# A second DRAM scratch holds v in float32 for units 1 to 3 of a block-sparse attention and FFN kernel, and the order of all engines is searched anew

## The chip, the cores and the metric

One core of one Trainium2 chip runs the whole program. The metric is the device time of one execution in microseconds; the kernel before was timed in three executions, and one execution was profiled.

## The reference

Attention of 4 batches, 8 heads, 768 tokens and head size 64, restricted to blocks of 32 tokens: a query block sees itself and its two neighbours, the first and the last block, and three sampled blocks of its own; the first and the last block see everything. Sampled blocks may repeat one another or a block that is seen anyway, and then count once. The result, as 3072 tokens by 512, goes through a two-layer network with an ELU between 512 to 2048 and 2048 to 512.

```python
scores = scale * np.matmul(q, k.transpose(0, 1, 3, 2))
mask = np.abs(blk_i - blk_j) <= window
mask = mask | (blk_i == 0) | (blk_j == 0) | (blk_i == n_blocks - 1) | (blk_j == n_blocks - 1)
...
        for kb in sampled_blocks[qb]:
            mask[qb * block:(qb + 1) * block, kb * block:(kb + 1) * block] = True
scores = np.where(mask, scores, -1000000000.0)
scores = scores - np.max(scores, axis=-1, keepdims=True)
attn = np.exp(scores)
attn = attn / (np.sum(attn, axis=-1, keepdims=True) + 1e-09)
out = np.matmul(attn, v)
...
x = out.transpose(0, 2, 1, 3).reshape(B * S, H * D)
h = x @ w_in
g = np.where(h > 0.0, h, alpha * (np.exp(np.minimum(h, 0.0)) - 1.0))
return g @ w_out
```

## The kernel before

**Units.** The batches are taken in two pairs. A unit is 128 tokens: two query blocks of both batches of a pair. Each pair has 12 units, the first of which holds the first and the last block; 24 units in all. Unit 0 (the code's `nat`) attends to all keys and goes in four parts of two heads each. Units 1 to 3 take their scores in float32, and units from 4 on work in float16 pairs: an f32 number is held as a high and a low half, and a product is three f16 matmuls (high by high, high by low, low by high).

**v.** `first_values` loads v of the first pair in three pieces of two tiles (`in_v_dram` into the room `wo`, 512 KB a tile), splits it into high and low halves in a tile `VT` (casts for the highs, L607 on DVE for the lows, scaled by 32, with columns of ones that give the row sums), and stores that as rows of 4160 bytes into a DRAM scratch `vd` (L681). A unit's two `VT` tiles are then loaded back from `vd`: the rows of the first and last block (32 partitions each), the window (96 rows), and an indirect DMA from GpSimd that gathers the 96 rows of the three sampled blocks by the index table `idx`. The tile of spare room is called `GR` in the trace and serves unit 1, the `VT` rooms serve units 0, 2 and 3 and what follows. Sampled rows that must not count are pointed by `idx` at a row of zeros in the scratch.

**p.** Unit 0 multiplies an f32 transpose of exp's output with v as it was loaded (64 columns a product). For units 1 to 3 the transposed p is split into high and low halves, some of the lows by a matmul that subtracts the high in PSUM (`pm`, for the first `LP[u]` tiles) and a copy, the others by a subtraction on DVE; the product with v (L1076) is f16, of 130, 66 or 64 columns.

**Weights.** The 16 tiles of 1 MB of the two layers go from DRAM into staging rooms (L548, L552; the list `STAGE`), and each is turned into high and low halves: a cast (ACT or DVE), a merge on DVE (L563), a second cast, and a subtraction on GpSimd or DVE (L570). The rooms `wi` and `wo` are where the finished halves stay too; k and v as loaded lie in the halves of `wo`. The kernel runs both layers of units 0 to 3 together (`ffn_two`: layer 1 is L1173, layer 2 is L1199), tile by tile of the weights, and of the later units pair by pair of units (`ffn`).

**What sets the order.** Nothing is issued by hand. Every step is put down in a `Plan` as an operation with a cost on each engine that can run it, a DMA cost, a due time (`prio`) and buffers out of rooms of a fixed number; a list scheduler in the program then fixes engine and order. A table of numbers, `RANK`, shifts due times, says how many weight loads wait for which mark (`HOLD`), and which tiles take which form (`LP`, `AP`, `LX`). All DMAs but the gathers, instruction fetches and the like are issued by SP in one queue, so that what stands ahead of a load in that queue, and waits, holds it up.

## Time and profile before

| what | value |
|---|---|
| three executions | 725.29, 733.63, 734.4 us (median 733.63) |
| profiled execution, its own time | 729.91 us |
| its span, from the first to the last instruction | 728.2 us |
| busy: PE, DVE, ACT, POOL | 679.6, 444.5, 449.9, 161.9 us |
| mean granted TensorE clock | 0.968 |
| moved by DMA | 123.18 MB, mean 169 GB/s |

The own time lies 1.7 us above the span, and 3.7 us under the median. Busy times are counted over the whole span, in which stages follow one another: attention of units 0 to 3 with the preparation of keys, values and weights (up to about 124 us), then a long stage in which layers of one pair of units run beside the attention of the next.

### The profile page before, as it was taken

To read this page: it belongs to the slowest core of one execution; us is meant where nothing else is said; L and a number is where in the kernel's file an instruction comes from. 1 tells how busy PE (TensorE), PEld (TensorE's weight loads), DVE (VectorE), ACT (ScalarE), POOL (GpSimd) and SP (SyncE) were. 2 spreads that over 40 slices of the span, in tenths; PEclk is the share of its full clock that TensorE was granted. 3 is DMA by queue.
4 is the path that set the end of the run, shared out by engine and by line. 5 is a ranking of instruction groups with operands and counts; after the bars stand their busy time and mean duration, and the time that the engine had idled before them with its cause. 6 is when DMAs were issued, how large, how long until landed. Compare 5 with 4: busy or idle time off the path is not lost.

```text
span 728.2 us, 23487 instructions
## 1 busy us (share of the span) xinstructions
PE 679.6 (93%) x9637; PEld 456.5 (63%) x9637; DVE 444.5 (61%) x882; ACT 449.9 (62%) x872; POOL 161.9 (22%) x357
## 2 busy tenths in 40 slices
...
PEclk9777978999999999999999999999999999999999
...
GB/s 211 259 321 240 284 282 196 237 182 212 177 193 163 152 199 203 164 202 187 135 139 181 184 201 142 173 219 122 104 150 203 149 198 135 145 60 15 16 1 29
DMA packets 213500, 123.18 MB, mean 169 GB/s; under 512 B 180560, under 2 KB 197072, under 8 KB 213008
## 3 DMA queue, kind: packets, MB, share of 16 engines
...
HBM read 76.98 MB, written 13.21 MB: 124 GB/s over the span
## 4 chain that ended last, share of the span: by engine, by line
PE 81%; DMA 10%; DVE 3%; ACT 2%; issue 1%; POOL 1%; POOLq 1%; another core or an unknown queue 0%; SPq 0%; DVEq 0%; ACTq 0%
PE h L1173 32%; PE o L1199 29%; PE av L1076 6%; DMA VT<-vd,idx 3%; PE s L1199 3%; PE s L996 2%; DMA VT<-vd 2%; PE s L987 2%; DMA wi<-in_moe_w_out_dram 2%; DMA GR<-vd 1%; PE av L1199 1%; PE warm L449 1%; DMA wo<-in_v_dram 1%; PE s L975 1%; PE s L503 1%
## 5 line engine op out<-in xcount | busy, mean ns | idle before, releaser
L1173 PE MATMUL h<-xT,wi 128*128 128x256 f16 x2304 | 264.7, 273 | 4.8 <-DVE FE L1181 4.3
L1173 PEld LDWEIGHTS <-wi 128*128 128x128 f16 x2304 | 221.9, 98 | 43.0 <-issue 8.6
L1199 PE MATMUL o<-wo,GR 128*128 128x512 f16 x1008 | 230.4, 379 | 1.7 <-ACT ro L405 1.7
L1199 PEld LDWEIGHTS <-GR 128*128 128x128 f16 x1152 | 108.9, 98 | 125.8 <-issue 6.4
L927 POOL COPY kG<-kT 128x128 int32 x264 | 91.0, 382 | 232.0 <-PE s L996 103.0
L1181 DVE SCALAR_TENSOR_TENSOR FE<-h,FE 128x512 f32<-128x512 f32 x96 | 66.0, 687 | 65.7 <-ACT FE L1186 65.7
L1013 DVE TENSOR_REDUCE m<-s 128x2 f32<-128x512 f32 x120 | 73.6, 648 | 35.5 <-PE s L996 20.0
L1184 ACT ACTIVATE FE<-h 128x512 f32<-128x512 f32 x96 | 56.8, 592 | 42.7 <-PE h L1173 31.6
L1191 DVE TENSOR_TENSOR GR<-FE,GR 128x512 f16<-128x512 f32 x93 | 66.1, 711 | 26.2 <-ACT GR L405 25.1
L797 DVE TENSOR_TENSOR p<-e,p 128x512 f16<-128x512 f32 x81 | 55.6, 690 | 39.0 <-ACT p L405 36.4
L761 ACT ACTIVATE e<-s,m 128x256 f32<-128x256 f32 x176 | 72.1, 475 | 9.1 <-DVE p L797 7.3
L880 POOL DMA_INDIRECT VT<-vd,idx x42 | 43.7, 1040 | 139.4 <-PE av L1076 107.7
L405 ACT ACTIVATE kG<-kT 128x384 f32<-128x384 f32 (+1 forms) x88 | 55.3, 678 | 25.7 <-PE s L996 14.2
L1186 ACT ACTIVATE FE<-FE,gs 128x512 f32<-128x512 f32 x96 | 69.4, 723 | 2.1
L1076 PEld LDWEIGHTS <-pT 128*32 128x32 f16 (+1 forms) x3432 | 41.9, 101 | 29.1 <-issue 26.9
L405 ACT ACTIVATE GR<-FE 128x512 f16<-128x512 f32 x64 | 40.2, 628 | 28.8 <-DVE FE L1181 28.7
L1076 PE MATMUL av<-VT,pT 128*32 128x66 f16 (+3 forms) x3288 | 47.3, 207 | 9.0 <-DMA VT<-vd,idx 6.9
L405 ACT ACTIVATE p<-e 128x512 f16<-128x512 f32 x70 | 43.6, 625 | 15.4 <-DMA pT<-p 15.3
L405 ACT ACTIVATE ro<-o 128x512 f32<-128x512 f32 x20 | 11.9, 597 | 58.0 <-PE o L1199 57.9
L987 PE MATMUL s<-kG,qT 64*32 64x256 f32 x704 | 27.2, 393 | 1.1 <-DVE pT L791 0.6
L405 ACT ACTIVATE kT<-s 128x1024 f16<-128x1024 f16 (+1 forms) x16 | 14.6, 914 | 20.9 <-PE s L503 11.5
L407 DVE COPY low<-av 128x192 f32<-128x192 f32 x28 | 10.0, 355 | 27.9 <-PE av L1076 25.3
...
## 6 DMA issues: line engine op xcount, KB each, us to landing
...
```

The lines of the kernel that those rows point to most:

```text
L405: nc.scalar.activation(dst, src, AF.Copy, scale=scale)
L761: nc.scalar.activation(e32.ap[:, y, :], s.ap[:, y, :], AF.Exp, bias=m.ap[:, 6 + y : 7 + y], scale=SC, accum_out=m.ap[:, 2 + y : 3 + y] if ...
L797: plan.add(LO, rank + 1, margin=mo, fn=lambda e: ENG[e].tensor_tensor(p.ap[:, 1, :], got(), p.ap[:, 0, :], op=ALU.subtract), r=[e32, p], w ...
L927: nc.gpsimd.tensor_copy(dst[:, :, r * W : (r + 1) * W], src[:, :, bass.ds(at[r], W)])
L1013: nc.vector.tensor_reduce(m.ap[:, at + i.start : at + i.stop], ss[c].ap[:, i], axis=AX.X, op=ALU.max, negate=True)
L1076: nc.tensor.matmul(av[half].ap[rs, at : at + w], lhsT=pts[d].ap[:, pl * 4 + y * 2 + z, rs], rhs=room[:, z, x, h * VW + v0 : h * VW + v0 + ...
L1173: nc.tensor.matmul(h.ap[:, a, :], lhsT=w[:, wl, cs], rhs=x.ap[:, xl, cc, :], start=(n == 0), stop=(n == 3 * NCC - 1))
L1181: nc.vector.scalar_tensor_tensor(e32.ap, h.ap, -IH * GS, e32.ap, op0=ALU.mult, op1=ALU.min)
L1184: plan.add({"ACT": 0.6}, p0, lambda e: nc.scalar.activation(e32.ap, h.ap, AF.Exp, scale=IH), r=[h], new=[e32], name=f"a1{U}.{f2}")
L1186: plan.add({"ACT": 0.72}, p0, lambda e: nc.scalar.activation(e32.ap, e32.ap, AF.Relu, bias=gs_col, scale=-GS), r=[e32], w=[e32], name=f"a2 ...
L1191: plan.add(LO, p0, margin=mo, fn=lambda e: ENG[e].tensor_tensor(g.ap[:, 1], e32.ap, g.ap[:, 0], op=ALU.subtract), r=[e32, g], w=[g], name= ...
L1199: nc.tensor.matmul(o.ap, lhsT=g.ap[:, gl, f % 2, m * P : (m + 1) * P], rhs=wo[:, part, wl, (f % 2) * DM : (f % 2 + 1) * DM], start=(f == 0 ...
```

## The change

- `raw_values` loads v and stores it at once, as float32, in a second scratch `vr` of 384 rows of 8 KB: a row is two tokens of both batches, all heads. Six stores of 512 KB follow the loads in SP's queue.
- Units 1 to 3 load their tiles from `vr`: two edges of 16 rows, a window of 48 rows, a gather of 48 rows by a new table `pair`, all of 8 KB. Their p is transposed and copied as float32 only (`pf`), without halves, and the product with v is float32, 192 matmuls of 64 columns over the three units in place of 480 of float16.
- What must not count is masked in the scores: one matmul with one row (bf16, K = 1) for each 32 queries adds either 0 or -1e30 per key block (`never`, `once`) before the scores, 48 of them in all. Row sums come from exp's accumulator.
- The tables for this are made by some 26 more small DVE operations at the start; `pair` stands beside `idx`.
- The split of v for `vd` (`first_values`) goes behind unit 0 in due time; its highs may go to POOL, its lows stay on DVE.
- k is staged in the rooms `wi` instead of halves of `wo`. Unit 0's scores wait for the keys of their own head pair only, its odd parts use other PSUM banks (`o`, `av`, `h`), and its maxima are combined by one reduction.
- `RANK` is searched anew, with new keys: `VR`, `VP`, `VW`, `AE`, `MT`, `LATE`, `FX`.

```diff
@@ -21,15 +21,16 @@
 WINDOW = 1
 
 RANK = {
-    "K": -1408.04, "Z": 990.23, "VL": 323.4, "Q": [1459.32, 294.42, 1902.98, -915.37, 340.37,
-    -247.43, 21.55, 1498.28, 151.89], "AT": [-1283.19, 1037.72, -509.33, 271.53, 54.11, 1021.44,
...
+    "K": 138.1, "Z": -56.04, "VL": 54.81, "VR": 368.88, "Q": [109.82, 906.62, -138.61, 751.86,
+    253.1, 41.87, 432.83, 499.33, 227.65], "AT": [339.57, -227.94, 84.04, 317.22, 14.82, 102.85,
...
+    "BACK": 1.72, "AHEAD": 17.2, "T": 36.02, "LEAD": 96.31, "V1": 106.51, "K1": -283.79, "MU":
+    5.06, "MI": 10.61, "MJ": -7.07, "MV": -2.76, "MP": -31.65, "AP": [0, 0, 0, 0], "AQ": 22.41,
+    "VP": 611.21, "VW": 536.9, "AE": -32.96, "MT": 216.47, "LATE": [-12.75, -6.78, -21.79],
+    "FX": {},
 }
...
+    NF, NPE = 4, 4
+    NEVER = 1.0e30
...
-    cols = const([1, NPAIR, (NB - 2) * NR], I32, "cols")
+    cols = tabs[0:1, 0:NC].rearrange("p (g n) -> p g n", g=NPAIR)
+    pair = tabs[:, NC : NC + NU2]
+    ONE = slice(P // 2, P // 2 + 1)
+    never = tabs[ONE, 0 : NU2 * (NR + 5) // 2].bitcast(BF16).rearrange("p (a b) -> p a b", b=NR + 5)
+    once = tabs[ONE, NU2 * (NR + 5) // 2 : NU2 * (NR + 5) // 2 + BLK // 2].bitcast(BF16)
+    nc.gpsimd.memset(once, 1.0)
...
+        nc.vector.tensor_tensor(d3, few[ONE], me[ONE, 1 : 1 + NU2].unsqueeze(2).to_broadcast([1, NU2, NR]), op=ALU.subtract)
...
+                nc.vector.tensor_tensor(d3[:, :, g], few[ONE, :, g], few[ONE, :, r], op=ALU.not_equal)
+                nc.vector.tensor_tensor(ok3[:, :, g], ok3[:, :, g], d3[:, :, g], op=ALU.mult)
+        nc.vector.memset(never, 0.0)
+        nc.vector.memset(never[:, 0, NR + 2 : NR + 3], -NEVER)
+        nc.vector.tensor_scalar(never[:, :, 0:NR], ok3, -1.0, NEVER, op0=ALU.add, op1=ALU.mult)
...
+        nc.vector.tensor_scalar(pair, w6, gk, None, op0=ALU.add)
...
-    STAGE = [(wi, 6), (wi, 4), (wi, 2), (wo, 6), (wo, 4), (wi, 6), (wi, 4), (wo, 6), (wo, 4), "g2",
+    STAGE = [(wi, 6), (wi, 4), (wi, 2), (wi, 6), (wi, 4), (wo, 6), (wi, 6), (wi, 4), (wo, 4), "g2",
...
-            s = halves[2 * hp + x]
+            s = wi_room[2 * hp + x]
...
-    def first_values(a, js, prio, load, write):
+    def raw_values(a, js, load):
+        for x in range(2):
+            s, t = staged(js[x], v[x], a, load, f"v0.{a}")
+            v_raw.append((s, t))
+
+            def put(e, x=x, s=s):
+                nc.sync.dma_start(
+                    vr.ap[a * P : (a + 1) * P, x * 2 * DM : (x + 1) * 2 * DM], s.ap.bitcast(F32))
+            new = (a, x) == (0, 0)
+            mark["vr"] = plan.add({"SP": 0.43}, RANK["VR"] + a, put, r=[s], new=[vr] if new else [], w=[] if new else [vr],
+                     dma=1.45, name=f"v2.{a}", pk=128)
+
+    def first_values(a, prio, write):
         def slot():
-            assert next_slot() == a
-            return VT[:, 2 * a : 2 * a + 2].rearrange("p c b (h x) -> p c b h x", h=H)
+            i = next_slot()
+            in_room["v", i] = None
+            return VT[:, 2 * i : 2 * i + 2].rearrange("p c b (h x) -> p c b h x", h=H)
         n = Buf("VT", slot)
         plan.add({"POOL": 0.5}, prio - 3, lambda e: nc.gpsimd.memset(
             n.ap.rearrange("p c b h x -> p (c b h) x")[:, :, D : D + 2], 1.0), new=[n], name=f"v10.{a}", port=False)
         for x in range(2):
-            s, t = staged(js[x], v[x], a, load, f"v0.{a}")
-            v_raw.append((s, t))
+            s, t = v_raw[2 * a + x]
             for c in range(2):
                 split(prio, s, n, lambda x=x, c=c: n.ap[:, c, x, :, 0:D],
-                      lambda x=x, c=c: n.ap[:, c, x, :, D + 2 :], VS, False, f"v0.{a}", t[:, :, c, :], mh=RANK["MV"])
+                      lambda x=x, c=c: n.ap[:, c, x, :, D + 2 :], VS, False, f"v0.{a}", t[:, :, c, :], mh=RANK["MV"],
+                      cost=({**CAST, "POOL": 1.0}, 0.69))
...
                 nc.sync.dma_start(
                     vd[0].ap[row : row + 2 * (p1 - p0), :].rearrange("(p c) e -> p (c e)", c=2),
                     n.ap[p0:p1].rearrange("p c b h x -> p (c b h x)"))
-            mark["vs"] = plan.add({"SP": 0.43}, write, put, r=[n], w=[vd[0]], dma=2.9 * (p1 - p0) / P, name=f"vs0.{a}",
+            plan.add({"SP": 0.43}, write, put, r=[n], w=[vd[0]], dma=3.2 * (p1 - p0) / P, name=f"vs0.{a}",
                      pk=256 * (p1 - p0) // P)
...
                         start=i == 0, stop=i == 3)
             tp = rank + 2
-            plan.add({"PE": 0.9}, tp, turn, r=[e32], new=[pt], code=8, name=f"pt{u}.{n}p")
-            if sums:
-                plan.add({"ACT": 0.6, "DVE": 0.66}, tp, lambda e: scaled(e, flat(pT.ap).bitcast(F32), flat(pt.ap)),
-                         r=[pt], new=[pT], margin=RANK["MP"], name=f"pf{u}.{n}", port=False)
-                return pT
...
+                        if in_room.get(("v", vt.slot)) != "raw":
+                            in_room["v", vt.slot] = "raw"
+                            for a, n in enumerate((0, NB - 1)):
+                                nc.sync.dma_start(
+                                    tile_[(NR + a) * HB : (NR + a + 1) * HB], vr.ap[n * HB : (n + 1) * HB, :])
+                        nc.sync.dma_start(tile_[(NR + 2) * HB :], vr.ap[(i - 1) * HB : (i + 2) * HB, :])
+                        return
...
-                plan.add({"SP": 1.5 if whole else 0.6}, tv, load, r=[vd[g]], new=[vt], dma=2.45 if whole else 1.5,  slack=RANK["SLACK"][2], name=f"vt{u}", nd=3 if whole else 1)
+                cost = (1.9 if whole else 1.15) if whole_f else 2.7 if whole else 1.62
+                plan.add({"SP": 1.5 if whole else 0.6}, tv, load, r=[vr if whole_f else vd[g]], new=[vt], dma=cost, slack=RANK["SLACK"][2], name=f"vt{u}", nd=3 if whole else 1)
 
                 def gather(e, i=i, vt=vt):
+                    if whole_f:
+                        n = NR * BLK // 2
+                        nc.gpsimd.indirect_dma_start(
+                            room32(vt.slot)[0:n], None, vr.ap, bass.IndirectOffsetOnAxis(ap=pair[0:n, i - 1 : i], axis=0))
+                        return
...
-                mark["vt", u] = plan.add({"POOL": 1.0}, tv, gather, r=[vd[g]], w=[vt], dma=1.65, slack=RANK["SLACK"][2], name=f"vg{u}")
...
+            ss = [buf(tag, [P, 2, 256], F32, ps) for tag in (("o", "av", "h") if nat and part % 2 else ["s"] * len(tiles))]
...
                 if wide_k:
                     q32 = flat(qT.ap).bitcast(F32).rearrange("p (h t) -> p h t", h=H // 2)
+                    for y in range(2 if whole_f else 0):
+                        for j, (rs, x) in enumerate(groups):
+                            nc.tensor.matmul(
+                                ss[y].ap[rs].rearrange("p i (z n t) -> p (i z) n t", z=2, t=BLK // 2), lhsT=once,
+                                rhs=never[:, i0 + j % 2 - 1].unsqueeze(1).unsqueeze(3).to_broadcast([1, 4, NR + 5, BLK // 2]),
+                                start=True, stop=False)
...
+                                kk, dst = kG32[rows, part, j % 2, 2 * i + x, :], ss[y].ap[rs, i, :]
+                                if whole_f:
+                                    kk = kk.rearrange("p (t z) -> p z t", z=2)
+                                    dst = dst.rearrange("p (z t) -> p z t", z=2)
                                 nc.tensor.matmul(
-                                    ss[y].ap[rs, i, :], lhsT=q32[rows, 2 * part + i, rs],
-                                    rhs=kG32[rows, part, j % 2, 2 * i + x, :], start=True, stop=True)
+                                    dst, lhsT=q32[rows, 2 * part + i, rs], rhs=kk, start=not whole_f, stop=i == 1 or not whole_f)
...
-            plan.add({"PE": 1.3 if nat else 1.1 if sp else 0.9 if wide_k else 0.7}, at_s, wide if sp else scores,
-                     r=[qT, *kT_any, *([kT_head[part]] if nat else kT_head), *kin[part : part + 1]],
-                     new=ss, code=20 if nat else 72 if sp else 32 if wide_k else 96, name=f"s{u}.{part}")
+            if nat:
+                for one in range(2):
+                    plan.add({"PE": 1.2 if one else 0.43}, at_s, lambda e, wide=wide, one=one: wide(e, turns=turns[:4] if one else turns[4:]),
+                             r=[qT, kT_head[part]], new=[] if one else ss, w=ss[:2] if one else [], code=16 if one else 4, name=f"s{u}.{part}")
...
+            if nat:
+                plan.add({"DVE": 0.42}, at_s + 0.5, lambda e, mm=mm, ss=ss: nc.vector.tensor_reduce(
+                    mm.ap[:, 2:3], ss[2].ap[:, 0:1], axis=AX.X, op=ALU.max, negate=True), r=[ss[2]], new=[mm],
+                    name=f"mx{u}.{part}", port=False)
+                plan.add({"PE": 0.43}, at_s + 0.4, lambda e, wide=wide: wide(e, turns=[(1, 2, 2, 1)]),
+                         r=[qT, kT_head[part]], w=[ss[2]], code=4, name=f"s{u}.{part}")
...
+                            nc.vector.tensor_reduce(
+                                m.ap[:, 6:8], m.ap[:, 0:6].rearrange("p (y c) -> p y c", c=3), axis=AX.X, op=ALU.min)
+                            return
...
-                sums = Buf(None, None) if nat else None
+                sums = Buf(None, None) if whole_f else None
+                if whole_f and not nat and c == 0:
+                    total = buf("r", [P, 4], F32)
...
+                        if whole_f:
                             for z in range(2):
-                                for rs, x in groups:
+                                for j, (rs, x) in enumerate(groups):
+                                    raw = v_raw[2 * k + x][1] if nat else room32(vin[j % 2].slot).rearrange(
+                                        "p (b h c d) -> p b h c d", b=2, h=H, c=2)[:, x]
                                     nc.tensor.matmul(
                                         av[half].ap[rs, at : at + D],
                                         lhsT=flat(pts[d].ap).bitcast(F32).rearrange("p (i t) -> p i t", t=P)[:, y * 2 + z, rs],
-                                        rhs=v_raw[2 * k + x][1][:, h, z, :], start=begin, stop=(d, y, z, 1) == end)
+                                        rhs=raw[:, h, z, :], start=begin, stop=(d, y, z, 1) == end)
...
+                    if whole_f:
                         nc.vector.tensor_scalar(r.ap, r.ap, PS * 1e-9, 1.0 / VS, op0=ALU.add, op1=ALU.mult)
                         nc.vector.reciprocal(r.ap, r.ap)
...
     zero_rows(RANK["Z"])
     for a in range(NB // 8):
-        first_values(a, (2 * a, 2 * a + 1), RANK["W"], RANK["VL"] + a, RANK["W"])
+        raw_values(a, (2 * a + 2, 2 * a + 3), RANK["VL"] + a)
...
+            plan.group = "vs"
+            for a in range(NB // 8 if u == 0 else 0):
+                first_values(a, RANK["VP"], RANK["VW"])
+            plan.group = "w"
```

SP's queue, from the second half of v's way to DRAM up to the first loads of tiles. Before (`vd_505` is the scratch of halves, `ST` a room with zero rows; `wi<-in_moe...` are weights):

```order
L681 DMA vd_505<-VT 128x4160
L681 DMA vd_505<-VT 112x4160
L681 DMA vd_505<-VT 16x4160
L552 DMA wi<-in_moe_w_out_dram 128x2x2047
L548 DMA wi<-in_moe_w_in_dram 128x4x1023
L872 DMA VT<-vd_505 32x2080
L873 DMA VT<-vd_505 32x2080
L874 DMA VT<-vd_505 96x2080
```

After (`vr_352` is the new scratch, `vd_590` the old one; `wi<-in_k_dram` are keys):

```order
L716 DMA vr_352<-wo 128x1024
L676 DMA wi<-in_k_dram 128x6x128 x2
L716 DMA vr_352<-wo 128x1024 x5
L800 DMA st_553<-in_q_dram 64x8x64 x2
L800 DMA st_572<-in_q_dram 64x8x64 x2
L639 DMA vd_590<-ST 32x2080
L932 DMA GR<-vr_352 16x2048 x2
L934 DMA GR<-vr_352 48x2048
L741 DMA vd_590<-VT 128x4160
L741 DMA vd_590<-VT 112x4160 x2
L741 DMA vd_590<-VT 16x4160 x2
```

The loads of the spare tile `GR` stood behind all stores of halves and behind weight tiles; now they stand behind the stores of raw v, two loads of q and the rows of zeros, and the stores of halves come after them.

The same queue where the last tiles of v for unit 3 and the first of unit 4 are loaded. Before:

```order
L552 DMA GR<-in_moe_w_out_dram 128x2x2047
L548 DMA wo<-in_moe_w_in_dram 128x4x1023
L874 DMA VT<-vd_505 96x2080 x2
L740 DMA st_1919<-in_q_dram 64x8x64 x2
L740 DMA st_1942<-in_q_dram 64x8x64 x2
L740 DMA st_1960<-in_q_dram 64x8x64 x2
L548 DMA wi<-in_moe_w_in_dram 128x4x1023
L702 DMA st_2136<-in_v_dram 128x8x64
L874 DMA VT<-vd_505 96x2080 x2
```

After:

```order
L934 DMA VT<-vr_352 48x2048
L939 DMA VT<-vd_590 32x2080
L940 DMA VT<-vd_590 32x2080
L941 DMA VT<-vd_590 96x2080
L594 DMA wi<-in_moe_w_in_dram 128x4x1023 x2
L598 DMA wo<-in_moe_w_out_dram 128x2x2047
L939 DMA VT<-vd_590 32x2080
L940 DMA VT<-vd_590 32x2080
L941 DMA VT<-vd_590 96x2080
```

Weights, q and window loads alternated; now whole tiles of `vd` (32, 32 and 96 rows) follow one another for unit 4 and on, with three weights between.

DVE, within unit 0's parts (`m` are maxima, `s`, `o`, `av`, `h` PSUM banks, `pT` transposed p). Before:

```order
L1013 TENSOR_REDUCE m_566<-s_542 128x2
L1013 TENSOR_REDUCE m_566<-s_544 128x1
L1013 TENSOR_REDUCE m_566<-s_543 128x2
L1013 TENSOR_REDUCE m_566<-s_544 128x1
L1027 TENSOR_TENSOR m_566<-m_566 128x2
L1028 TENSOR_TENSOR m_566<-m_566 128x2
L1035 TENSOR_SCALAR m_566<-m_566 128x2
L563 SCALAR_TENSOR_TENSOR wi<-wi,ZB 128x1024
L1044 TENSOR_TENSOR r_538<-m_566 128x2
L570 TENSOR_TENSOR wi<-wi 128x1024
```

After:

```order
L418 COPY pT_446<-h_435 128x512
L418 COPY pT_457<-h_441 128x512
L1094 TENSOR_REDUCE m_473<-h_462 128x1
L654 SCALAR_TENSOR_TENSOR VT<-wo,VT 128x8x64
L1107 TENSOR_REDUCE m_473<-o_460 128x2
L1107 TENSOR_REDUCE m_473<-av_461 128x2
L1107 TENSOR_REDUCE m_473<-h_462 128x1
L1094 TENSOR_REDUCE m_516<-s_480 128x1
L1130 TENSOR_REDUCE m_473<-m_473 128x2
L1107 TENSOR_REDUCE m_516<-s_478 128x2
L1141 TENSOR_SCALAR m_473<-m_473 128x2
```

The merge and the subtraction of a weight tile stood between the maxima of one part; now the low halves of v and copies of p stand there, and the maxima of two parts interleave.

## Rows read from the trace of the kernel before

**Rows 1.** The page: busy time of PE, and its granted clock in 40 slices.

```profile
PE 679.6 (93%) x9637; PEld 456.5 (63%) x9637; DVE 444.5 (61%) x882; ACT 449.9 (62%) x872; POOL 161.9 (22%) x357
...
PEclk9777978999999999999999999999999999999999
```

**Rows 2.** Windows by stage: per engine busy us and instructions, clock, DMA share, GB/s.

```profile
20.00:72.00 52.00, 33.37 (x394) 22.89 (x389) 30.73 (x70) 26.27 (x60) 10.38 (x21) 0.74 1.05 277
72.00:124.00 52.00, 38.39 (x822) 24.25 (x819) 36.47 (x76) 40.42 (x77) 18.07 (x43) 0.84 0.93 259
124.00:180.00 56.00, 55.56 (x598) 40.22 (x597) 51.42 (x75) 44.29 (x75) 20.38 (x26) 1.00 0.87 213
262.00:700.00 438.00, 432.39 (x6396) 295.21 (x6395) 262.63 (x529) 278.57 (x538) 81.20 (x189) 1.00 0.77 147
```

**Rows 3.** The chain that ended last: start, us, what; its longest DMA steps.

```profile
20.11 6.60 DMA wo<-in_v_dram
...
38.99 14.21 DMA wi<-in_moe_w_out_dram
53.23 16.73 DMA VT<-vd
69.97 10.81 DMA GR<-vd
...
101.35 9.87 DMA VT<-vd,idx
```

**Rows 4.** Timeline of PE, 0 to 140 us.

```profile
22.48 1.57 PE L956 MATMUL s<-kT,qT 64*64 64x256 f32 x20 [1.41 <-ACT qT L405]
...
39.56 1.62 PE L1064 MATMUL av<-wo,pT 128*64 128x64 f32 x48
...
111.25 2.15 PE L1076 MATMUL av<-VT,pT 128*32 128x130 f16 x103 [3.91 <-DMA VT<-vd,idx]
...
123.69 5.41 PE L1173 MATMUL h<-xT,wi 128*128 128x256 f16 x48
```

**Rows 5.** Timeline of DVE, 0 to 125 us.

```profile
6.98 0.18 DVE L481 TENSOR_TENSOR odd<-odd 128x24 f32<-128x24 f32 x1
...
21.79 0.69 DVE L607 SCALAR_TENSOR_TENSOR VT<-wo,VT 128x512 f16<-128x512 f32 x1
...
58.88 1.22 DVE L563 SCALAR_TENSOR_TENSOR wi<-wi,ZB 128x1024 int32<-128x1024 int32 x1
...
69.93 1.29 DVE L1013 TENSOR_REDUCE m<-s 128x2 f32<-128x512 f32 x2 [1.08 <-PE s L987]
...
72.21 0.42 DVE L1101 TENSOR_TENSOR x<-av,r 128x256 f32<-128x256 f32 x1 [0.51 <-PE av L1064]
```

**Rows 6.** Timeline of ACT, 8 to 140 us.

```profile
44.12 1.34 ACT L405 ACTIVATE ZB<-wi 128x1024 f16<-128x1024 bf16 x1 [4.40 <-DMA wi<-in_moe_w_in_dram]
45.34 0.66 ACT L756 ACTIVATE FE<-s,m 128x512 f32<-128x512 f32 x1
```

**Rows 7.** Windows by what the DMA queues move; columns as in rows 2.

```profile
11.00:14.00 3.00, 3.00 (x60) 3.00 (x58) 0.00 (x0) 2.17 (x4) 0.00 (x0) 1.00 1.17 294
42.00:50.00 8.00, 3.86 (x26) 2.77 (x28) 2.61 (x3) 5.52 (x12) 0.00 (x0) 0.61 1.01 391
57.50:79.50 22.00, 18.90 (x264) 13.21 (x264) 13.17 (x30) 17.30 (x38) 4.22 (x15) 0.77 1.04 242
0.00:176.00 176.00, 141.68 (x2019) 98.42 (x2020) 122.32 (x240) 117.41 (x221) 55.57 (x113) 0.87 0.94 245
```

**Rows 8.** Timeline of POOL, 0 to 140 us.

```profile
1.75 0.54 POOL L433 TENSOR_SCALAR odd<-ident 128x128 f16<-128x128 f32 x1
...
134.69 1.99 POOL L797 TENSOR_TENSOR p<-e,p 128x512 f16<-128x512 f32 x1 [5.34 <-ACT p L405]
```

**Rows 9.** Timelines of SP's queue, DVE and PE, 165 to 262 us: the last weight tile.

```profile
176.05 0.37 SPq L552 DMA_DIRECT2D ST<-in_moe_w_out_dram  x1
...
190.23 2.18 DVE L570 TENSOR_TENSOR wo<-ST,wo 128x1024 f16<-128x1024 f32 x1
...
202.77 1.46 PE L1199 MATMUL av<-wo,GR 128*128 128x512 f16 x6
```

186 lines of the change are left out of this document (118 added, 68 removed), and 11 rows, old and new, of the table RANK.

## The prediction

> **What bounds the kernel now.** I read the page first: PE is busy 679.6 of 728.2 us, and its granted clock is under nine tenths only within the first seven of 40 slices [rows 1]. The windows by stage then split the span: from 262 to 700 us PE is busy 432.39 of 438 at full clock, from 124 to 180 us 55.56 of 56, but from 20 to 72 only 33.37 of 52 and from 72 to 124 only 38.39 of 52 [rows 2]. So the place where time can be won is the first 124 us. The timeline of PE gives the border: at 123.69 the first long run of layer 1 begins (48 matmuls), and from there PE hardly waits [rows 4]. The work behind it is the same in both programs: units 0 to 3, the first scores of unit 4, the tiles h and o of layers 1 and 2 that lie ahead of this run lie ahead of it in the new order too. I call the moment at which PE gets there S; the new time is the old one plus the shift of S, so long as nothing later starves.
>
> What sets S is told by the chain of waits: its long links ahead of S are DMA, 6.60 us for v, 14.21 for a weight tile, 16.73 and 10.81 for tiles from `vd`, 9.87 for the gather of unit 3 [rows 3]. A link of 16.73 us is not a transfer: a tile is 0.4 MB in loads and as much in the gather, some 0.8 to 1.05 MB, 4.3 us at the 242 GB/s that this stage moves [rows 7]; the rest is queueing behind weights. Besides, DVE is busy 30.73 of 52 us in the first stage and 36.47 in the second, yet 51.42 of 56 in the next [rows 2]; unit 0 ends on it only at 72.21 [rows 5]. The load before S is therefore shared by the DMA queues and a DVE that waits for them.
>
> **Unit 0.** The new order loads k, v and q0, 6.6 MB, at the start; at 294 GB/s [rows 7] these take 22.6 us and land at about 25. The 26 table operations more cost 26 x 0.18 = 4.7 us of DVE, by the row at 6.98 [rows 5] (8 us if the one-row forms come with 0.3 us each, which no row shows). They run while k is still landing, and before the scores of unit 0, at 22.48 in the old trace [rows 4]; I cost them at nothing; uncovered they would cost their 4.7 to 8.
>
> In unit 0 the old DVE order had two operations of a weight tile between the maxima of a part, and ACT held an exp at 45.34 behind a cast that had waited 4.40 us for a weight tile [rows 6]. In the new order no weight tile stands ahead of unit 0's last exp. DVE's work in it: 16 large and small maxima, at 1.29/2 = 0.65 us for a large one [rows 5], 8.5 us together; 12 copies of p at most 0.65, 7.8; 12 lows of v at 0.69 [rows 5], 8.3; small operations and norms 4; in all 29 us. DVE worked at 59% in the window 20 to 72 and at 92% in 124 to 180 [rows 2]. Unit 0's chain of score, maximum, exp, transpose, product now has two sets of banks, so I take 75%, in the middle: 38 us from 15, an end at 53 (46.5 at 92%, 64 at 59%) in place of 72.
>
> **v's way.** Old: v landed, was split, stored, and came back behind weights. New, from the order of SP's queue: six stores of raw v (3.1 MB, at the 391 GB/s of the window 42 to 50 [rows 7], 8 us) end at 33; q1 and q2 at 36; the first raw tile of unit 1 (1.05 MB with its gather, 4.3 us at 242) at 40; the halves of v for `vd` (3.1 MB) at 48; the second raw tile at 53, as unit 0 ends; three more raw tiles (12.9) at 71 behind the first weight; three weights, the sixth raw tile and the first `vd` tile by 89; three weights by 97, two `vd` tiles by 106, then unit 4's transposes by about 112. The extra traffic is the store of raw v, 3.1 MB (12.7 us of DMA at 245 GB/s [rows 7], 8 at 391), less 0.4 MB or so of narrower tiles; it is paid in a stretch in which weights waited before.
>
> **Units 1 to 3 on PE.** 480 f16 products at 2.15/103 = 21 ns [rows 4], 10.0 us, go; 192 in f32 at 1.62/48 = 34 ns [rows 4], 6.5 us, come (half of it at full clock). The 48 mask products of 512 columns cost 48 x 1.46/6 = 11.7 us if each takes a whole pass as the 512-column rows of layer 2 do [rows 9], 2.9 if the four groups of 32 queries run beside each other; no row shows a product of one row. I take 6, half way. PE's sum ahead of S thus moves by -3.5 + 6 = +2.5 (-4 to +8), against 13.6 us of idle time in 72 to 124 [rows 2]: hidden, except where a mask sits on the chain of a unit, a few tenths. Lows of p leave DVE and PE, accumulated row sums cost ACT a little.
>
> **S.** Between unit 0's end and S, DVE has 50 us of work in the new order (weights up to the sixth tile with merges at 1.22 [rows 5], units 1 to 3, unit 4's halves); 5 us of it overlap unit 0's end. 45 us at 85% (70% as in 72 to 124, 92% as in 124 to 180 [rows 2]) is 53 us: S at 106, with 95 to 128 from the joint ends of the two stages. The DMA sum gives 106 for the `vd` tiles and 112 for unit 4's transposes; PE has other work for all but 2 to 3 us of that. So S = 108, 15.7 us ahead of 123.69. Behind it the last weight must come in time: issued at 176.05, converted at 192.4, used at about 200 to 204 [rows 9]; the new sum of traffic up to there is 46.9 in place of 43.1 MB, 15.7 us more at 245 GB/s, if weights were held up all the way; I count on most of it vanishing in idle DMA time and the 10 us of slack.
>
> The profiled execution took 729.91, its span 728.2: 728.2 - 15.7 + 1.7 = 714.2, and the median of the runs lies 3.7 higher, which a new median would share in part. I forecast **715**.
>
> **Rivals.** A, the split of v still gates (chance 0.08). Its highs may go to POOL; the nearest rows of POOL are 0.54 us for 128 columns and 1.99 for a 512-column operation [rows 8], so a cast may cost 2 to 3 us. Twelve of these put the stores of `vd`, and behind them in SP's queue the second raw tile, 13 us later: S 119, time 725. Against it: the first raw tile stands ahead of those stores, and nothing before unit 4 needs `vd`.
>
> B, narrow destinations (0.15). Tiles of 32 and 96 partitions moved 242 GB/s where loads of 128 partitions moved 391 [rows 7]; raw tiles arrive as 16 and 48 partitions. With the same ratio once more, 150 GB/s, a raw tile takes 7.0 us in place of 4.3, five whole tiles 13.5 us more, on the stretch where DVE waits for them: S about 120, time 726. [...]
>
> C, the slower side: weights come too late (0.10). If the 3.8 MB more and the loads that now stand ahead push the last weight by the full 15.7 us, it is issued at 192 and converted at 208. PE, which is 15 us earlier, would want it at 187: it waits 21 us, and the win turns into 736. It decides from an issue later than about 178. For it: whole weight tiles stand behind raw tiles and behind `vd` tiles; against it: the DMA share is 0.93 and 0.87 in these stages [rows 2], so part of the excess fits.
>
> D, DVE packs as in 124 to 180 (0.15): 92% in both stages gives unit 0 by 47 and S at 96 to 98, PE's wait for transposes included; time 704.
>
> **How the numbers follow.** Forecast 0.52 (707 to 722), A 0.08, B 0.15, C 0.10, D 0.15. The range leaves out half of C, a third of D and the tails: 703 to 733. A measurement of this kernel can tell about 2%, so the border of faster is 719: three quarters of the forecast's own chance falls below it, all of D is under it, none of A to C: 0.39 + 0.15 is 0.54, of which I move 0.06 to same, since the new runs may scatter over 9 us as the old ones did: faster 0.48. Slower by over 2% needs 748, further than C's 736, and would take C's lateness in the second layer too: 0.06. The rest, 0.46, is same.
>
> **What the new profile would show.** The first long run of layer 1 at about 108 with PE hardly idle after it (wrong if it starts at 118 or later, or if PE idles again between 140 and 210 for `wo`, which is C). Unit 0's last norm at 53 (D: 47; over 62 means that its chain, and not DVE, sets it). The loads of raw tiles for unit 1 issued right behind the stores to `vr`, landed by 40 (B: 43 and later, the stretch of raw tiles under 200 GB/s). No wait of PE for a gather of `VT` ahead of S, where the old one waited 3.91 us at 111.25 [rows 4]. POOL's casts of v at 1 us or less (A: 2 to 3). DVE's busy share from 53 to 108 at 85%. The mask products between 60 and 240 ns each. The last weight issued by 178. The prediction fails if S hardly moves, because a chain within the units that no sum of busy time shows sets their pace, or if the gain at S is given back by late weights.

## The result and the profile after

The changed kernel takes 736.96 us in the median of 20 executions (733.35 to 741.65), the kernel before 728.4 in 20 on the same chip (725.05 to 735.17; the 733.63 above was the median of three). The ratio is 1.0125 [1.0101, 1.015]: about 1% slower, under the 2% at which it would count as slower, where I forecast 715 and gave 703 to 733. Medians are of all executions, and ratios leave out those that lie more than 1.5% over the fastest of their kernel, so a ratio need not be the quotient of the medians. The profiled execution took 734.94 us, with a span of 733.2. The medians thus lie 8.6 us apart and the spans 5.0; the rows below account for the 5.0.

The page of the kernel after shows no new idle time over the whole span: PE is busy for 5 us more in a span 5 us longer. Its granted clock is higher in the first slices than in [rows 1], ACT has less to do and POOL more.

```profile
PE 684.8 (93%) x9585; PEld 457.1 (62%) x9585; DVE 453.4 (62%) x886; ACT 397.4 (54%) x797; POOL 235.6 (32%) x457
...
PEclk9988798999999999999999999999999999999999
```

The timelines of DVE (two rows) and PE of the kernel after answer to [rows 4, 5]. Unit 0 ends at 56.6, not at 72.2; unit 2's last product ends at 90.6 (98.5 before); PE then waits 5.78 us for unit 3's gather; DVE sits idle 8.15 us for the scores behind it; and the long run of layer 1, S, comes at 122.74 in place of 123.69. The third block is the timeline of PE in the kernel before: the first scores of unit 1 and the last product of unit 2.

```profile
56.64 0.42 DVE L1214 TENSOR_TENSOR x<-av,r 128x256 f32<-128x256 f32 x1 [2.22 <-PE av L1175]
...
112.23 1.29 DVE L1111 TENSOR_REDUCE m<-s 128x2 f32<-128x512 f32 x2 [8.15 <-PE s L1070]
```

```profile
56.52 0.61 PE L1058 MATMUL s<-tabs 1*32 1x512 bf16 x8
57.06 1.13 PE L1070 MATMUL s<-kG,qT 64*32 64x256 f32 x32
...
89.49 1.10 PE L1175 MATMUL av<-VT,pT 128*32 128x64 f32 x64
...
108.38 1.93 PE L1175 MATMUL av<-VT,pT 128*32 128x64 f32 x62 [5.78 <-DMA VT<-vr,tabs]
...
122.74 5.65 PE L1287 MATMUL h<-xT,wi 128*128 128x256 f16 x35 [1.47 <-DVE xT L1268]
```

```profile
68.80 1.09 PE L987 MATMUL s<-kG,qT 64*32 64x256 f32 x32
...
96.99 1.50 PE L1076 MATMUL av<-VT,pT 128*32 128x66 f16 x96
```

So the 15.6 us that unit 0 wins are spent again before S. From unit 0's end to unit 2's last product the old kernel took 26.3 us and the new one takes 34.0 (+7.7); from there until the gather of unit 3 is down, 12.8 and 17.8 (+5.0); from there to S, 12.4 and 14.4 (+1.9). That leaves 1.0 us at S. Behind it 610.5 us follow in place of 604.5 (6.0 lost), and 6.0 - 1.0 is the 5.0 us by which the spans differ.

Half of the 7.7 is an overlap that is gone. The old order begins the scores of unit 1 at 68.80, 3.4 us ahead of unit 0's end; the new one begins them at 57.06, 0.4 us behind it. Counted from these scores, units 1 and 2 take 29.7 us in the old order and 33.5 in the new one.

The chain of waits of the kernel after (start, us, what; shown from 80 to 112 us) no longer has the links of [rows 3] for tiles from `vd` (16.73 and 10.81), but still a weight tile (11.54, in place of 14.21) and the gather (11.52, in place of 9.87):

```profile
80.56 11.54 DMA wi<-in_moe_w_out_dram
...
96.81 11.52 DMA VT<-vr,tabs
108.33 0.04 issue
108.38 1.93 PE av L1175 x62
```

The DMA view of the kernel after, cut to 56 to 112 us, has 40 slices of 1.4 us: busy share of the 16 engines in tenths, and what they moved.

```profile
DMA  8899999999999999999999999999999999999999
GB/s 242 244 203 361 370 162 183 187 152 158 176 181 181 176 258 157 151 120 177 307 385 387 395 415 331 189 173 152 241 136 213 272 341 268 176 177 202 379 405 352
```

The engines count as busy throughout, but from 63 to 75 us (slices 6 to 14) they move 152 to 187 GB/s. In this stretch three of the six raw tiles are loaded whole, six edges, three windows and three gathers, which SP and POOL issue between 58.1 and 67.9. A stage with full queues can thus move less than half of what it moves elsewhere (385 to 415 in slices 21 to 24); the forecast took 242 for it.

The windows of the kernel after, by stage (columns as in [rows 2]), with the stretch of raw tiles first:

```profile
57.00:72.00 15.00, 11.45 (x252) 7.67 (x249) 7.87 (x20) 6.59 (x20) 7.55 (x19) 0.89 1.03 221
57.00:108.00 51.00, 34.65 (x587) 20.34 (x583) 31.49 (x62) 24.60 (x63) 25.97 (x54) 0.85 1.05 233
124.00:180.00 56.00, 52.59 (x743) 37.48 (x742) 48.53 (x73) 42.83 (x73) 32.33 (x44) 0.97 1.02 244
180.00:262.00 82.00, 82.00 (x972) 52.42 (x971) 53.30 (x93) 45.34 (x86) 30.69 (x51) 1.00 0.92 198
262.00:700.00 438.00, 430.67 (x6309) 291.41 (x6308) 265.64 (x522) 247.39 (x498) 108.98 (x240) 1.00 0.76 148
```

DVE is busy 31.49 of 51 us (62%) between unit 0's end and the S that I forecast. Behind S, PE idles 3.4 us in 124 to 180 (0.44 before), has none in 180 to 262, and loses little in 262 to 700.

### The profile page after: what moved, and what is told of

Same layout as the page of the kernel before. It is cut to its first block, busy times and chain, and to the rows that moved or that the text cites. A ratio compares the mean times of both kernels' runs of the same rounds, so it can differ in the third digit from the quotient of the medians.

```text
span 733.2 us, 23439 instructions
## 1 busy us (share of the span) xinstructions
PE 684.8 (93%) x9585; PEld 457.1 (62%) x9585; DVE 453.4 (62%) x886; ACT 397.4 (54%) x797; POOL 235.6 (32%) x457
## 3 DMA queue, kind: packets, MB, share of 16 engines
q8 instruction: 75, 1.23, 0.7%
## 4 chain that ended last, share of the span: by engine, by line
PE 77%; DVE 7%; DMA 5%; issue 4%; ACT 2%; POOL 2%; SPq 1%; POOLq 1%; another core or an unknown queue 0%; ACTq 0%; DVEq 0%
PE h L1287 30%; PE o L1313 28%; PE av L1187 5%; PE s L1078 2%; PE s L1313 2%; PE s L1070 2%; PE av L1175 2%; DMA wi<-in_moe_w_out_dram 2%; DMA VT<-vr,tabs 2%; PE av L1313 1%; POOLq L996 1%; DMA wo<-in_v_dram 1%; DVE m L1111 1%; DVE p L849 1%; PE h L839 1%
## 5 line engine op out<-in xcount | busy, mean ns | idle before, releaser
L1111 DVE TENSOR_REDUCE m<-s 128x2 f32<-128x512 f32 x104 | 65.7, 664 | 43.8 <-PE s L1070 25.6
L849 DVE TENSOR_TENSOR p<-e,p 128x512 f16<-128x512 f32 x84 | 64.7, 771 | 25.3 <-ACT p L416 24.9
L953 POOL DMA_INDIRECT VT<-vd,idx x38 | 37.3, 980 | 115.5 <-PE av L1187 101.8
L1300 ACT ACTIVATE FE<-FE,tabs 128x512 f32<-128x512 f32 x96 | 69.4, 722 | 2.2
L1305 DVE TENSOR_TENSOR GR<-FE,GR 128x512 f16<-128x512 f32 x72 | 51.6, 718 | 26.4 <-ACT GR L416 25.0
L1305 POOL TENSOR_TENSOR GR<-FE,GR 128x512 f16<-128x512 f32 x24 | 34.6, 1442 | 58.5 <-DVE GR L418 31.8
L1187 PEld LDWEIGHTS <-pT 128*32 128x32 f16 (+1 forms) x2952 | 34.2, 97 | 14.3 <-issue 13.5
L1187 PE MATMUL av<-VT,pT 128*32 128x66 f16 (+5 forms) x2952 | 40.3, 203 | 0.0
L979 POOL COPY kG<-kT 128x384 int32<-128x384 int32 x68 | 39.7, 612 | 0.0
L1139 ACT ACTIVATE m<-m 128x2 f32<-128x2 f32 x79 | 15.6, 202 | 31.5 <-DVE m L1111 26.4
```

The lines of the kernel that those rows point to most:

```text
L849: plan.add(LO, rank + 1, margin=mo, fn=lambda e: ENG[e].tensor_tensor(p.ap[:, 1, :], got(), p.ap[:, 0, :], op=ALU.subtract), r=[e32, p], w ...
L1111: nc.vector.tensor_reduce(m.ap[:, at + i.start : at + i.stop], ss[c].ap[:, i], axis=AX.X, op=ALU.max, negate=True)
L1187: nc.tensor.matmul(av[half].ap[rs, at : at + w], lhsT=pts[d].ap[:, pl * 4 + y * 2 + z, rs], rhs=room[:, z, x, h * VW + v0 : h * VW + v0 + ...
L1300: plan.add({"ACT": 0.72}, p0, lambda e: nc.scalar.activation(e32.ap, e32.ap, AF.Relu, bias=gs_col, scale=-GS), r=[e32], w=[e32], name=f"a2 ...
L1305: plan.add(LO, p0, margin=mo, fn=lambda e: ENG[e].tensor_tensor(g.ap[:, 1], e32.ap, g.ap[:, 0], op=ALU.subtract), r=[e32, g], w=[g], name= ...
```

## Experiments

The first four runs were sent with two theories. **Bytes**: the traffic that the change adds, its store of raw v and its tiles, fills the queues. **Chain**: units 1 to 3 run at the pace of their own steps, and only the sixth tile is late; **masks**, that the one-row products weigh in these steps, is a part of it. **Narrow destinations** (rival B: loads of 16 and 48 partitions move slowly whatever else is under way) was put to the test after them, from `e8_rows` on. **Supply** (PE lacks instructions in runs of short products; by the pages of both kernels instructions come by DMA, in 75 packets of together 1.23 MB and 33 of 0.27) and **order** (the new table costs the later units time) came up for the loss behind S. S and spans are of the profiled execution, ratios are against the kernel before on the same chip. Where two or three kernels stand in one paragraph, the expectation of each is quoted.

**Quarter rows.** The tiles of units 1 to 3 are loaded with a quarter of the bytes, in `e1_quarter_both` with quarter stores too, in `e3_quarter_tiles` with the full stores.

```diff
-                        nc.sync.dma_start(tile_[(NR + 2) * HB :], vr.ap[(i - 1) * HB : (i + 2) * HB, :])
+                        nc.sync.dma_start(tile_[(NR + 2) * HB :, 0:DM], vr.ap[(i - 1) * HB : (i + 2) * HB, :])
...
-                            room32(vt.slot)[0:n], None, vr.ap, bass.IndirectOffsetOnAxis(ap=pair[0:n, i - 1 : i], axis=0))
+                            room32(vt.slot)[0:n, 0:DM], None, vr.ap, bass.IndirectOffsetOnAxis(ap=pair[0:n, i - 1 : i], axis=0))
```

> The order on every engine stays that of the changed kernel; the scratch vr holds only a quarter of each row (the first 512 numbers), the six stores write a quarter, the six raw tiles load a quarter, and units 1 to 3 multiply with that quarter for all heads, so their output is not the reference's. 2.4 MB of stores and 4.7 MB of tile loads are gone. Theory bytes (the DMA engines, busy at a share of 1.00 from the start to 172 us, set the pace, and the bytes that the change adds and the slow 8 KB rows ate what unit 0 gave): at 255 GB/s 7.1 MB are 28 us, of which the chain of units 1 to 3 lets perhaps 12 to 16 through; the first long run of layer 1 moves from 122.7 to 107 to 111 and the time from 737 to about 723. Theory chain (units 1 to 3 run one after the other, each at the pace of its own steps, and the tiles are there in time but for the sixth): only the 5.8 us wait for the sixth gather goes, the run begins at 116 to 118 and the time is about 732.

> As the run before (a quarter of each raw row is loaded and used, output not the reference's), but the six stores write all 3.1 MB, in pieces of 2 KB. Theory bytes: the 4.7 MB of tile loads are worth 10 us and the 2.4 MB of stores the rest, so the first long run of layer 1 begins at 110 to 114, some 3 us or more behind the kernel with quarter stores, time about 727. Theory chain: the same as with quarter stores within 1 us, 116 to 118, time about 732, since nobody waits for the stores.

Both: 726.3 us, ratio 0.9983 [0.9943, 1.0023], S 114.52. Tiles alone: 729.15, ratio 0.9981 [0.9926, 1.0036], S 113.20, and no wait for the gather ahead of S is left. The loads of the tiles are worth 9.5 us of S and about 1.4% of the time; smaller stores bring nothing beyond them. S of the quarter tiles lies where **bytes** put it (110 to 114), not where **chain** did (116 to 118), but the stores, for which **bytes** expected 3 us or more, do not hold it up. Whether the tiles cost by their bytes or by the partitions that they land in, these two runs cannot tell.

**Stores twice** (`e4_double_store`), to see what the cover of the store is worth.

```diff
                 nc.sync.dma_start(
                     vr.ap[a * P : (a + 1) * P, x * 2 * DM : (x + 1) * 2 * DM], s.ap.bitcast(F32))
+                nc.sync.dma_start(
+                    vr.ap[a * P : (a + 1) * P, x * 2 * DM : (x + 1) * 2 * DM], s.ap.bitcast(F32))
```

> The changed kernel with every store to vr issued twice (3.1 MB more of the very traffic that the change adds, output unchanged, same order). Theory bytes: 3.1 MB at 255 GB/s are 12 us, the first long run of layer 1 moves from 122.7 to 131 to 135 and the time to 745 to 749. Theory chain: the raw tiles of unit 1 come up to 8 us later but still before or little after unit 0's end at 57, so the run moves by 0 to 4 us, time 737 to 741.

756.0 us, ratio 1.0391 [1.0314, 1.0467], S 140.09: S is 17 us later than in the kernel after, for 3.1 MB that account for 8 to 12.7 us at the rates of [rows 7], and the time is above what either theory expected. The edit does more than add traffic: a second store writes the same bytes as the first, and SP's queue waits for the first to land before it issues it. The waits of SP's queue from 20 to 57 us (us in total, times, longest):

```profile
SPq L718 <- DMA vr<-wo: 22.2, 6, 4.9
```

Rows of PE's timeline in this kernel show how this reaches PE: unit 0's last transposes stand behind transposes of q for a later unit, which wait for q, behind the stores in the queue, and unit 1 waits for the raw tile, which must wait for the last store.

```profile
58.14 1.09 PE L877 MATMUL o<-ident,st 128*128 128x128 f32 x4 [6.21 <-DMA st<-in_q_dram]
...
78.21 1.07 PE L1177 MATMUL av<-GR,pT 128*32 128x64 f32 x30 [6.15 <-DMA GR<-vr]
```

So the run shows what 22 us of waiting in SP's queue cost, and not what 3.1 MB more would cost beside the other traffic; how much of the store's cover is left was not measured.

**No masks** (`e2_no_mask`).

```diff
-                    for y in range(2 if whole_f else 0):
+                    for y in range(0):
...
-                                    dst, lhsT=q32[rows, 2 * part + i, rs], rhs=kk, start=not whole_f, stop=i == 1 or not whole_f)
+                                    dst, lhsT=q32[rows, 2 * part + i, rs], rhs=kk, start=True, stop=True)
```

> The changed kernel without the 48 one-row mask products of units 1 to 3 (duplicates are then counted twice, so the output is not the reference's); same order. Theory bytes: PE's time is not what binds before the sixth gather, the first long run of layer 1 moves by 0 to 1 us, time 736 to 737. Theory chain: the masks stand in each part's chain of score, maximum, exp, at 0.54 to 1.0 us for eight, six times, so unit 2's end, and with it the sixth gather, come 3 to 4 us earlier, run at 119, time about 733.

737.52 us, ratio 1.0146 [1.0075, 1.0217], S 120.87. Eight masks take 0.61 us on PE in the rows above, 76 ns each. To leave them out brings S forward by 1.9 us, where **chain** expected 3 to 4, and does not make the kernel measurably faster. **Masks** falls as the cause.

**The loads by themselves** (`e8_rows`). A kernel of 121.79 us loads v from DRAM, four loads to a case, and DVE waits for each case to land. (A write of zeros to the output, 0.8 MB beside each, runs under the first four cases.)

```python
    def case(parts, width=2048, src=rows):
        fence()
        for c in range(4):
            ...
                nc.sync.dma_start(big[sl, c, 0:width], src[lo : lo + n, :])
...
    case([slice(0, 16)])
    case([slice(0, 48)])
    case([slice(80, 128)])
    case([slice(0, 64, 4)])
    case([slice(0, 128, 8)])
    case([slice(0, 128)])
```

> A kernel of loads alone (its output is zeros): four loads of v, then a fence, for each of: 16 partitions 0 to 15 of 8 KB; 48 partitions 0 to 47; 48 partitions 80 to 127; 16 partitions at every fourth of 64; 16 at every eighth of 128; all 128; 48, 128, 32 and 96 partitions of 4 KB; 48 partitions as three loads at every third; four gathers of 48 partitions of 8 KB. Theory of narrow destinations (a row of 8 KB took 680 to 860 ns in the changed kernel because few partitions in a row are written at a time): 16 partitions in a row show over 700 ns a row and under 200 GB/s, 128 show about 320 ns a row and 400 GB/s, and partitions spread over 64 or 128 lie between or near the latter. Rival (rows are slow there because weights, transposes and gathers of other queues run beside them): alone, every case shows 310 to 330 ns a row, and the rates differ only by the time of start and end.

The timeline of DVE in this kernel: the figure in brackets is the time of the case that ends there. In this order: 16 rows of 8 KB in a row of partitions, 48, 48 at the upper end, 16 on every fourth partition, 16 on every eighth, all 128; the last one is four gathers of 48 rows.

```profile
16.76 0.06 DVE L377 MEMSET big<- 128x4 f32 x1 [6.69 <-DMA big<-in_v_dram]
29.43 0.06 DVE L377 MEMSET big<- 128x4 f32 x1 [12.60 <-DMA big<-in_v_dram]
42.19 0.06 DVE L377 MEMSET big<- 128x4 f32 x1 [12.70 <-DMA big<-in_v_dram]
47.05 0.06 DVE L377 MEMSET big<- 128x4 f32 x1 [4.79 <-DMA big<-in_v_dram]
51.88 0.06 DVE L377 MEMSET big<- 128x4 f32 x1 [4.77 <-DMA big<-in_v_dram]
64.34 0.06 DVE L377 MEMSET big<- 128x4 f32 x1 [12.40 <-DMA big<-in_v_dram]
...
119.03 0.06 DVE L377 MEMSET big<- 128x4 f32 x1 [14.28 <-DMA big<-in_v_dram,idx]
```

Forty-eight partitions take as long as 128 (12.60 and 12.40 us), with 3/8 of the bytes. Without zeros beside them, the same 48 rows sent as three loads of every third partition took 13.35 us; of rows of 4 KB, 48 took 6.65 us, 128 took 7.76, 32 took 4.29 and 96 took 7.99. The same 16 rows take 6.69 us side by side and 4.79 spread. Between these cases of one row length the time goes with where the rows lie, and not with the bytes alone. By these rows a window of 48 rows costs 12.6/4 = 3.2 us, a gather 14.28/4 = 3.6, an edge 6.69/4 = 1.7: 6.7 us for a raw tile without edges and 10 with them, for which I had put 4.3 on the path.

Why 48 partitions take the time of 128 no run here shows.

**The same bytes over all partitions** (`e12_even`): as many loads and gathers of the same size, each spread over 128 partitions.

```diff
-                        nc.sync.dma_start(tile_[(NR + 2) * HB :], vr.ap[(i - 1) * HB : (i + 2) * HB, :])
+                        nc.sync.dma_start(tile_[:, 512:1280], even(768)[128 * i : 128 * (i + 1), :])
...
-                            room32(vt.slot)[0:n], None, vr.ap, bass.IndirectOffsetOnAxis(ap=pair[0:n, i - 1 : i], axis=0))
+                            room32(vt.slot)[:, 1280:], None, even(768), bass.IndirectOffsetOnAxis(ap=pair[:, i - 1 : i], axis=0))
```

> The changed kernel, same order, same number of DMAs and same bytes, but each load of a raw tile is spread over all 128 partitions (edges 128 x 1 KB, window and gather 128 x 3 KB) in place of 16 or 48 rows of 8 KB; what lands in the tile is then not the keys' rows, so the output is not the reference's. In the run of loads alone 48 rows of 8 KB took as long as 128 rows (12.7 and 12.5 us for four). [...] Theory bytes (what the quarter tiles saved was their bytes, whatever the partitions): the run stays at 120 to 123 and the time at 735 to 738.

The run that is meant there is S. **Narrow destinations** expected it at 111 to 115, as with the quarter tiles, and the time at 727 to 730.

724.29 us, ratio 1.0001 [0.9959, 1.0043], S 112.98 (in an execution of 719.05 us). The window of the raw tiles in this kernel has 324 GB/s where the kernel after has 221, and of the wait for the gather 1.04 us are left; the third row is S.

```profile
57.00:72.00 15.00, 10.44 (x232) 7.12 (x232) 7.99 (x19) 7.24 (x20) 7.73 (x19) 0.87 1.07 324
```

```profile
100.10 0.86 PE L1178 MATMUL av<-VT,pT 128*32 128x64 f32 x42 [1.04 <-DMA VT<-vr,tabs]
...
112.98 3.98 PE L1290 MATMUL h<-xT,wi 128*128 128x256 f16 x35 [1.46 <-DVE xT L1271]
```

With the bytes, the number of DMAs and the order unchanged, 9.8 us of S and 1.2% of the time hang on which partitions the rows land in. The rows are shorter too, 1 and 3 KB in place of 8, but the two cases of 16 rows of 8 KB differ in the partitions alone (6.69 and 4.79 us). **Narrow destinations** stands, for the part ahead of S. It is not the whole loss: S comes 10.7 us earlier than in the kernel before, and the time is only equal to it.

**Runs of short products.** In the first profile after, f16 scores of the later units have nine pauses of up to 0.5 us, 3.7 us in all, that nothing in the profile explains. `e11_spread` swaps neighbours on PE so that a run of products with v doesn't stand right ahead of scores; `e13_even_spread` does so on top of the even tiles; `e9_phase32` and `e10_phase64` shift the whole program by more matmuls in the warm-up.

```diff
+    def apart(self, done):
+        ...
+            if not (s.name[0] == "s" and s.code == 96 and x.name[0] in "ho" and s.start > 150):
+                continue
...
+            seq.remove(x)
+            seq.insert(at, x)
```

```diff
-        for i in range(32):
+        for i in range(64):
```

(`e10_phase64` has 96 there.)

> The changed kernel in which, at the places where 72 products av and 48 f16 scores follow each other on PE (or with 12 matmuls h between), the next h or o of PE's order is put ahead of the scores, if all it needs was issued before; output unchanged, all else in the same order. Theory supply (PE runs out of instructions after some 110 short matmuls in a row, in gaps of 0.4 to 0.7 us that begin at the same matmul whatever the number of instructions ahead): the gaps behind the first long run go from 9.5 us to under 4, and the time by 4 to 7 us, to 730 to 733. Rival keys (the scores wait for kG at these places): the gaps shrink only by what the move delays the scores, 1 to 2 us, and the time by less than 2.

> Both edits together (output not the reference's because of the spread rows). If narrow loads and the short matmuls in a row are the two losses, and independent, the gains add: 13 to 16 us under the changed kernel, 721 to 724, some 5 us under the kernel before. If one of them is a story, the time is that of the other edit alone.

> The changed kernel with 32 more small matmuls in the warm-up (64 more PE instructions, 0.5 us, before the first key has landed); order and output unchanged. In the changed kernel the f16 scores of the later units take 27.7 us behind the first long run of layer 1 in place of 18.9 before, in gaps of 0.4 to 0.7 us inside a group that no semaphore explains (9 waits, 3.7 us). Theory supply (PE waits for its own instructions, which come in blocks counted from the start): the gaps change place or number, the sum moves by several us, up or down, and with it the time, by 2 to 5 us. Rival keys (scores wait for kG, whose copies have moved to POOL): the gaps stand at the same matmuls of the same groups, time 737 as the changed kernel.

> As the run before with 64 more small matmuls (128 more PE instructions, 1.0 us). Theory supply: another set of gaps, the time moves by 2 to 5 us against both the changed kernel and the run before. Rival keys: the same gaps at the same matmuls, time 737 to 738.

Spread: 732.25, ratio 1.0154 [1.0074, 1.0234]; even and spread: 723.74, ratio 0.9982 [0.9936, 1.0029], against 1.0001 for even alone. Shifted: 743.6, ratio 1.0202 [1.0108, 1.0296], and 745.03, ratio 1.0207 [1.0136, 1.0279], with the pauses at the same matmuls, so they don't hang on the number of instructions ahead. The swap does not test **supply**, because it had no pauses to remove: they stand in each profile of the new program from the first chip, chip 14 (the first four runs) and chip 1 (the shifted ones), nine to eleven of them, and in none from chips 11 and 5, `e12_even` without the swap and `r_after` among them. What makes them stays open. They are not the whole loss either: without them the spread kernel is at 1.0154.

**Both kernels again** (`r_before`, `r_after`), on another chip, unedited.

> The kernel before once more, for a profile on the same chip as the three runs beside it. Ratio 1.00; first long run of layer 1 at 122 to 125; from there to the end 603 to 607 us as in its first profile (604.5). If the profiles scatter as the times do (some 4 us either way), this stretch comes out anywhere from 600 to 609.

> The changed kernel once more. Ratio 1.0125; first long run at 121 to 124, and from there to the end 608 to 616 us (610.5 in its first profile), with the gaps in the f16 scores of the later units. Rival scatter: 603 to 607 here, as long as in the kernel before on this chip, and a ratio that rests on the stretch ahead of the run.

Before: 724.09, ratio 0.9953 [0.9906, 0.9999], which is how far from 1 the same program can come out; its profile, of an execution of 732.67 us, has S at 123.64 and 607.3 us behind it. After: 731.08, ratio 1.0089 [1.0047, 1.0131]. Here the kernel after, in a profiled execution of 737.91 us, the longest of its ten, has its S at 125.70 and again 610.5 us behind it, without the nine pauses, but with a wait that the first profile does not have, seen in PE's timeline:

```profile
433.63 8.46 PE L1287 MATMUL h<-xT,wi 128*128 128x256 f16 x60 [4.84 <-DMA xT<-n]
```

**Order.** `e16_sched` gives the six numbers of the new table that concern the later units their old values (the sixth, `AQ`, goes from 22.41 to 25.47); `e18_w_early` brings three weight tiles forward in the plan.

```diff
-    "BACK": 1.72, "AHEAD": 17.2, "T": 36.02, "LEAD": 96.31, "V1": 106.51, "K1": -283.79, "MU":
...
+    "LX": [1, 0, 0, 0], "BACK": 1.72, "AHEAD": 78.49, "T": 64.92, "LEAD": 117.53,
+    "V1": 256.9, "K1": 76.71, "MU": 5.06, "MI": 10.61, "MJ": -7.07,
```

```diff
-    "FX": {},
+    "FX": {'wl0': -600.0, 'wl8': -600.0, 'wl1': -600.0},
```

> The changed kernel with the six keys that place the units from 4 on (T, LEAD, AHEAD, V1, K1, AQ) as they were before; PE's order is the same up to its row 993 of 15904, SP's up to its row 58, some 117 us. Theory order (the new order of the later units loses the time behind the first long run): from that run to the end 603 to 607, time 5 to 9 us under the changed kernel on this chip, ratio 1.000 to 1.006. Rival weights: the same loss stays, ratio 1.010 to 1.015, since weights come and are converted as late as in the changed kernel.

> The changed kernel with the first three weight tiles moved ahead in the plan: two of them are loaded ahead of the stores to vr, one ahead of the first raw tile; what follows is planned anew. Theory weights: three tiles less to convert behind the first long run, PE's busy time in the 56 us behind it rises from 52.6 to 55 or more, and the stretch to the end falls by 3 to 6 us; the run itself comes 0 to 8 us later, since 3 MB more stand ahead of the raw tiles; ratio 1.006 to 1.02. Rival order: the stretch behind the run stays at 609 to 612.

Old numbers: 748.12, ratio 1.0332 [1.025, 1.0414], S 119.65, and 626 us behind it. Weights early: 766.7, ratio 1.0543 [1.0467, 1.062], S 136.36, and 632 us behind it. **Order** expected 603 to 607 behind S from the old numbers, and its rival a ratio of 1.010 to 1.015; neither came. The new numbers suit the new program better than the old ones, and weights that come earlier cost much ahead of S and save nothing behind it. So these six numbers are not the cause, and an earlier start of the weights is no remedy. The order that the scheduler makes behind S is not the old one in either run, so that it costs time is not excluded.

## Why the prediction was wrong

**Right: where time can be won, unit 0, the masks, the hidden store.** The first 124 us were the place where time could be won. Unit 0 ends at 56.6 (forecast 53, 72.2 before). Masks took 76 ns, within 60 to 240. Operations of the tables on one row took 0.16 us each (L512 and L513, 1x6), not 0.3. The store costs nothing that can be measured: beside quarter tiles, a quarter of it is no faster than all of it (ratios 0.9983 and 0.9981, S 114.52 and 113.20). From one form of the new program to another a shift of S reaches the end: in `e3_quarter_tiles` S is 9.5 us earlier than in the kernel after and the span 9.2 us shorter.

**The step that failed: the price of a raw tile, "1.05 MB with its gather, 4.3 us at 242".** I took the rate from tiles that land in 32 and 96 partitions [rows 7] and used it for 16 and 48. Loads into 48 partitions take the time of loads into 128 (12.60 and 12.40 us for four, `e8_rows`), which is 6.7 us a tile, and 10 with edges. Rival B had both the cause, narrow loads, and nearly the price, 7.0 us, and I gave it 0.15. Its S of 120 is close to the 122.7 measured; its time, 726, is not, for it too lost nothing behind S. The forecasts that follow from the step fell with it: no wait of PE for a gather of `VT` ahead of S (5.78 us), DVE at 85% (62%: it waits for the tiles, as before), S at 108. S moved by 1.0 us, which is the first of the signs by which the prediction was to fail. Of the 14.7 us by which S is late, the even tiles give 9.8 back. The other 5 us are two terms of the sum: unit 0's end, 55.5 there in place of 53, and "45 us at 85%". In the kernel with even tiles DVE has 42.3 us of work between 55.5 and 113, so the work was sized well, but it is done in 57.5 us, a share of 74%:

```profile
55.50:72.00 16.50, 11.94 (x265) 7.63 (x264) 8.39 (x20) 7.24 (x20) 7.73 (x19) 0.88 1.05 317
72.00:113.00 41.00, 31.46 (x545) 17.38 (x532) 33.93 (x60) 26.28 (x61) 26.53 (x49) 0.88 0.91 251
```

The stages of the old reckoning take 31.3, 13.3 and 12.9 us there: the last two are those of the kernel before to half a microsecond, and the first is 5.0 us longer even when the tiles are not late. Of these, 3.8 are the overlap that is gone: unit 1's scores begin at 55.91 there, 0.4 us behind unit 0's end, and 3.4 ahead of it in the old order; from these scores on units 1 and 2 take 30.9 us, 1.2 more than before. "5 us of it overlap unit 0's end" was a term without a row, and no run shows it: in the kernel after, DVE has no maximum of unit 1 before 58.24 and no merge of a weight before 68.17.

A count was wrong as well. The f32 products of units 1 to 3 are not 192 but 384 (L1175 in the trace, 128 with `GR` and 256 with `VT`), 13.1 us at the forecast's 34 ns in place of 6.5. From 57 to 124 us they take 10.92: 17 ns each where the granted clock is 1.00 (64 in 1.10 us at 89.49) and 31 where it is 0.50 (62 in 1.93 at 108.38). PE is busy for 90.5 us up to S in the kernel after and for 89.8 before, so the count alone does not explain the late S.

**The second step that failed: "The work behind it is the same in both programs", and with it "the new time is the old one plus the shift of S".** S came 1.0 us earlier, and the time is 8.6 us longer by the medians, 5.0 by the spans. 610.5 us follow S in both profiles of the kernel after, against 604.5 and 607.3 before. Three things were seen. First, the granted clock: in the kernel after the first 35 matmuls take 5.65 us, 161 ns each, where the even tiles have 3.98 for the same 35 and the kernel before 5.41 for 48 [rows 4], 113 ns. That is 1.7 us. The windows right behind S of the kernel after, and of the kernel before, show it in the third figure from the end, the granted clock (0.66 and 1.00):

```profile
122.70:126.00 3.30, 3.26 (x20) 2.46 (x20) 2.47 (x2) 2.72 (x3) 3.30 (x6) 0.66 1.00 224
```

```profile
123.70:127.00 3.30, 3.30 (x35) 2.96 (x32) 3.30 (x5) 3.30 (x9) 1.44 (x4) 1.00 0.73 157
```

Ahead of S, from 114 to 122.7, the clock is 1.00 and PE is busy for 5.09 of 8.70 us. In `e10_phase64` PE is busy for 5.40 of 8.80 us ahead of S, with the same waits, and the 35 matmuls take 3.98 us, 114 ns each; so idle time ahead of S does not settle it, and what does is not shown.

```profile
120.84 3.98 PE L1287 MATMUL h<-xT,wi 128*128 128x256 f16 x35 [1.46 <-DVE xT L1268]
```

Second, weights are late, as C had it, but PE does not wait for them: by 124 us six merges of weights (L609) are done where eight were (L563), and the last weight tile is issued at 187.46 us (forecast 178, 176.05 before). Yet of PE's idle time in 124 to 180 (3.4 us in place of 0.44) most is for DVE's part of the ELU, `FE`, and none for a weight, as the waits of PE from 123 to 212 us show; whether DVE is late with `FE` because of the weights was not tried.

```profile
PE h L1287 <- DVE FE L1295: 3.1, 3, 2.5
```

From 180 to 262 PE is busy for all of the 82 us, where the kernel before has 78.98, so that much is caught up:

```profile
180.00:262.00 82.00, 78.98 (x1092) 49.78 (x1091) 54.29 (x106) 48.03 (x105) 25.10 (x55) 1.00 0.91 177
```

Third, the f16 scores of the later units, behind S: busy time, mean ns and idle time before them, of the kernel after and of the kernel before.

```profile
L1078 PE MATMUL s<-kG,qT 64*32 64x256 f16 x1056 | 22.9, 271 | 5.7 <-issue 3.7 <-ACT e L819 0.9 <-POOL kG L979 0.7
```

```profile
L996 PE MATMUL s<-kG,qT 64*32 64x256 f16 x1056 | 19.3, 271 | 0.2 <-POOL kG L927 0.2
```

These are 9.1 us more, above the 6.0 lost in this profile, against 3.0 us of waiting for a gather (L1076) that are gone. But in the second profile of the kernel after they take 19.8 and 2.0, and the same 610.5 us follow S, with 4.84 for `xT` among them. With even and spread tiles 608.5 us follow S, with quarter tiles 610.8, and with even tiles 604.3, though in an execution 5.2 us under its median; by the medians the even tiles, too, lose behind S what they win ahead of it. Neither the old numbers, nor early weights, nor the swap removed the loss for certain. What sets it stays open.

**What stays of the change.** Its own gain at unit 0 is 15.6 us; the narrow loads take 10 of them back and units 1 and 2 another 5, 4 of these because unit 1 no longer starts under unit 0's end; the loss behind S makes it 1% slower. With the tiles spread evenly it comes out equal to the kernel before, not ahead of it, and that layout doesn't hold the rows where the products need them; no version here beats both.

**The range.** It reached to 733 and the median is 737. B and the losses behind S were held to be rivals, each by itself; they came together, and no case of mine added them.
